# Prologue of a fused FFT filter and FFN: W_in loaded in seven pieces, x of batch 1 issued straight behind it, the imaginary filter cast on three engines, placements of F moved

## Chip, cores and metric

The kernel runs on one core of one Trainium2 chip. Times are device microseconds (us) of one execution. "Span" is the length of the profiled execution from its first to its last instruction; it is about 2 us shorter than that execution's time. Engines: PE (TensorE, matmuls), PEld (its weight loads), DVE (VectorE), ACT (ScalarE), POOL (GpSimd), SP (SyncE, which here issues the DMAs).

## The reference

```python
def _attn_ref(x, filt_r, filt_i):            # x: (8, 3008, 256), filters: (1505, 256)
    X = np.fft.rfft(x, axis=1)
    Y = X * (filt_r + 1j * filt_i)[None, :, :]
    return np.fft.irfft(Y, n=x.shape[1], axis=1).astype(np.float32)

def _moe_ref(x, w_in, w_out):                # x: (24064, 256), w_in: (256, 2048), w_out: (2048, 256)
    h = np.maximum(x @ w_in, 0.0)
    return (h * h @ w_out).astype(np.float32)
# reference: _moe_ref(_attn_ref(x, filt_r, filt_i).reshape(24064, 256), w_in, w_out)
```

## The kernel before

The Fourier transforms are matmuls. For each batch: a first transform (x to u, tile `psA`), u through memory (`dU`) into another order (`ut`), a second transform (`psB`), the product with the filter F (`prods`, `sF`), an inverse part (`psP`, evicted to `ze`), Z through memory (`dZ`, `zt`), a last inverse part (`psY` to `yt`). Then the FFN takes `yt` in groups of 512 tokens: `psH` = W_in times y, relu into `h`, square, `psO` = h times W_out. The FFN of one batch runs while the transform of the next is placed between its matmuls in a fixed order. Only batch 0, and three quarters of the first transform of batch 1, stand ahead of the FFN: that is the prologue, and only there does the change act.

The filters arrive with rows spread over partitions; `place_f` puts them in order with matmuls against permutation matrices and evicts the result to `sF`. `turn_u` does the same for u of batch 0 on chip.

```python
    def load_win(k):                       # W_in in two halves, in the buffers of x
        w32s[k] = p_x32.tile([128, DFF], F32, tag="x32", name=f"win32_{k}")
        nc.sync.dma_start(out=w32s[k], in_=moe_w_in[128 * k:128 * k + 128, :])

    def cast_win(k):
        for j in range(2):
            c = slice(1024 * j, 1024 * j + 1024)
            nc.gpsimd.tensor_copy(out=sWin[:, k, c], in_=w32s[k][:, c])
    # ... cut ...
    def unit_p0(k):                        # inverse part of batch 0: evict, write Z
        # ... cut: 8 matmuls into ps ...
        nc.scalar.copy(out=ze, in_=ps.rearrange("p t (a d) -> p (t a) d", d=D))
        nc.sync.dma_start(
            out=dZ[0].rearrange("(s p) d -> p s d", p=128)[:, 4 * k:4 * k + 4, :],
            in_=ze)
    # ... cut: the prologue ...
    for im, e in ((0, e0), (0, e1), (1, e0)):
        nc.gpsimd.tensor_copy(out=f16s[0][:, im, e], in_=f32s[im][:, e])
    # ... cut: sSPx, a copy of sSP with its halves swapped, on POOL ...
    for k in range(2):
        cast_win(k)
    uts[0] = p_ut.tile([128, NC, D], F16, tag="ut", name="ut_0")
    load_wide(1, 2)                        # x of batch 1, first third to be issued
    cast_wide(1, 2, nc.gpsimd, nc.gpsimd)
    for k in range(6):
        turn_u(k, nc.vector if k in (1, 3, 4, 5) else nc.scalar)
        if k > 2:
            place_f(0, k - 3, nc.scalar, True)
    nc.vector.tensor_copy(out=f16s[0][:, 1, e1], in_=f32s[1][:, e1])
    place_f(0, 3, nc.vector, True)
    place_f(1, 0, nc.scalar)
    for k in range(7):                     # "the loop"
        if k < 6:
            unit_b(0, 2 * k)
            if k < 5:
                place_f(1, k + 1, nc.scalar)
            unit_b(0, 2 * k + 1)
        if k > 0:
            unit_p0(k - 1)
        if k < 2:
            place_f(0, k + 4, nc.scalar)
        if k in (1, 2):                    # the other two thirds of x, behind writes of Z
            load_wide(1, k - 1)
            cast_wide(1, k - 1, nc.gpsimd, nc.gpsimd)
    read_z(0, 0)
    load_wout(0)
    read_z(0, 1)
    load_wout(1)
    for c in (0, 2, 1):
        chunk_a(1, c)                      # first transform of batch 1: 24 matmuls
    for c in (0, 2, 1):
        write_u(1, c)
    for n in range(4):
        unit_y(0, n)                       # first y, needs Z back from memory
    # ... cut: then the FFN, with the transforms of later batches between ...
```

## Time and profile before

| | before |
|---|---|
| median of 3 runs | 794.77 us (794.66 to 795.65) |
| the profiled execution | 797.61 us, span 795.8 us |
| PE busy | 783.1 us, 98% of the span |
| prologue, to the first relu `h` | 53.80 us |
| granted PE clock, 40 to 50 us | 0.66 |

### The profile page before, as it was taken

What the parts mean: (1) busy time and instruction counts of PE and PEld (TensorE: products, weight loads), DVE (VectorE), ACT (ScalarE), POOL (GpSimd) and SP (SyncE); (2) the same over time, 40 slices, a digit from 0 to 9 for tenths busy, and PEclk for the clock granted to TensorE, in tenths of its full rate; (3) what the DMA queues carried; (4) which work ended last, traced back from release to release, by engine and by line L of the source; (5) the groups of instructions that cost most, each with busy time, mean ns of one, the idle gap of its engine ahead of it and who ended that gap; (6) DMA issues with size and microseconds to landing.
All of it is one profiled execution on the core that took longest, in us unless ns stands there. A gap on an engine that the chain in (4) does not pass through costs nothing.

```text
span 795.8 us, 14801 instructions
## 1 busy us (share of the span) xinstructions
PE 783.1 (98%) x6102; PEld 553.7 (70%) x6102; DVE 552.2 (69%) x898; ACT 554.9 (70%) x708; POOL 24.4 (3%) x27
## 2 busy tenths in 40 slices
PE   8989999999999999999999999999999999999998
PEld 5846677667676676867778676776777667776666
DVE  6946995579855897559965699557985589554342
ACT  3856776767777677767777677676776767766664
POOL 3710000000000000000000000000000000000000
PEclk9989999999999999999999999999999999999999
DMA  9994555336724467055471555525563342511111
GB/s 352 361 277 134 130 151 139 92 126 165 202 58 107 158 165 181 30 164 151 124 183 49 171 153 137 129 71 156 156 170 97 87 142 80 123 48 41 40 41 54
DMA packets 88139, 107.32 MB, mean 135 GB/s; under 512 B 6288, under 2 KB 78864, under 8 KB 83856
## 3 DMA queue, kind: packets, MB, share of 16 engines
q1 hardware_dynamic: 87864, 106.19, 46.9%
q8 instruction: 48, 0.79, 0.4%
q10 hardware_dynamic: 144, 0.18, 0.1%
q14 instruction: 19, 0.16, 0.1%
q0 software_dynamic: 64, 0.00, 0.0%
HBM read 58.12 MB, written 48.23 MB: 134 GB/s over the span
## 4 chain that ended last, share of the span: by engine, by line
PE 93%; DMA 3%; ACT 1%; DVE 1%; issue 0%; POOL 0%; SPq 0%; ACTq 0%; DVEq 0%; POOLq 0%
PE psO L577 40%; PE psH L560 39%; PE psA L359 3%; PE psY L530 3%; PE psB L443 2%; PE psP L494 2%; PE warm L274 1%; DMA ut<-dU 1%; DMA xw<-in_x_dram 1%; PE psf L293 1%; DMA dZ<-ze 1%; ACT h L564 1%; PE psf L296 0%; DMA dU<-u 0%; PE psA L380 0%; ACT sF L303 0%
## 5 line engine op out<-in xcount | busy, mean ns | idle before, releaser
L564 ACT ACTIVATE h<-psH 128x1024 f16<-128x1024 f32 x376 | 385.2, 1025 | 189.7 <-PE psH L560 188.2
L577 PE MATMUL psO<-sWout,h 128*128 128x256 f16 x3008 | 388.6, 272 | 0.0
L560 PE MATMUL psH<-yt,sWin 128*128 128x512 f16 (+7 forms) x1728 | 386.9, 351 | 1.7 <-DVE yt L539 0.8
L577 PEld LDWEIGHTS <-h 128*128 128x128 f16 x3008 | 290.6, 98 | 77.3
L568 DVE TENSOR_TENSOR h<-h 128x1024 f16<-128x1024 f16 x376 | 253.7, 685 | 100.8 <-ACT h L564 99.2
L560 PEld LDWEIGHTS <-sWin 128*128 128x128 f16 x1728 | 159.5, 98 | 101.7 <-issue 3.5
L451 DVE TENSOR_TENSOR prod<-psB,sF 128x1024 f16<-128x1024 f32 x84 | 102.4, 1219 | 5.9 <-PE psB L443 5.6
L539 DVE CAST yt<-psY 128x376 f16<-128x376 f32 x62 | 33.9, 549 | 57.4 <-PE psY L530 57.4
L365 DVE CAST u<-psA 96x512 f16<-96x512 f32 x50 | 34.3, 687 | 47.3 <-PE psA L359 45.1
L496 ACT CAST ze<-psP 128x512 f16<-128x512 f32 x84 | 49.2, 586 | 17.8 <-PE psP L494 15.9
L588 ACT COPY ost<-psO 128x512 f32<-128x512 f32 (+1 forms) x96 | 55.7, 580 | 6.7 <-PE psO L577 5.3
L530 PEld LDWEIGHTS <-zt 112*128 112x128 f16 x512 | 34.9, 98 | 12.1 <-issue 2.0
L530 PE MATMUL psY<-sC,zt 112*128 112x94 f16 x512 | 42.3, 205 | 0.6 <-DMA zt<-dZ 0.3
L465 DVE TENSOR_TENSOR yf<-prod,yf 128x512 f16<-128x512 f16 x84 | 35.7, 425 | 2.9
L443 PE MATMUL psB<-ut,sSB 128*128 128x256 f16 x192 | 36.5, 272 | 0.6 <-DMA ut<-dU 0.5
L359 PE MATMUL psA<-x,sC 94*96 94x512 f16 x96 | 36.6, 382 | 0.0
L443 PEld LDWEIGHTS <-sSB 128*128 128x128 f16 x192 | 18.6, 98 | 20.9 <-issue 1.7
L494 PE MATMUL psP<-yf,sSP 128*128 128x256 f16 x168 | 32.1, 273 | 0.2 <-ACT yt L537 0.2
L537 ACT CAST yt<-psY 128x376 f16<-128x376 f32 x66 | 30.7, 468 | 1.1 <-PE psY L530 0.6
L338 DVE CAST x<-x 94x2048 f16<-94x2048 f32 x24 | 29.2, 1216 | 0.0
L363 ACT CAST u<-psA 96x512 f16<-96x512 f32 x50 | 28.6, 572 | 0.0
L458 DVE COPY yf<-prod 64x512 f16<-64x512 f16 x84 | 24.3, 289 | 2.9
(63 smaller groups left out, 255.9 us busy)
## 6 DMA issues: line engine op xcount, KB each, us to landing
x<-in_x_dram SPq DMA_DIRECT2D x20, 768.0 KB
zt<-dZ SPq DMA_DIRECT2D x64, 192.0 KB
dU<-u SPq DMA_DIRECT2D x28, 384.0 KB
dZ<-ze SPq DMA_DIRECT2D x28, 384.0 KB
out_dram<-ost SPq DMA_DIRECT2D x66, 128.0 KB
out_dram<-ost SPq DMA_DIRECT2D x31, 256.0 KB
ut<-dU SPq DMA_DIRECT2D x7, 1024.0 KB
xw<-in_x_dram SPq DMA_DIRECT2D x4, 1024.0 KB
```

What stands on the lines that cost most here:

```text
L359: nc.tensor.matmul(ps[0:96, :], sSA, x16s[(b, c)][:, m, :], start=True, stop=True)
L443: nc.tensor.matmul(ps[:, i * D:(i + 1) * D], sSB[:, 2 * p + i, :], uts[b][:, 2 * p + i, :], start=True, stop=True)
L451: nc.vector.tensor_mul(out=prod, in0=ps.rearrange("p (a d) -> p a d", d=D).unsqueeze(1).to_broadcast([128, 2, 2, D]), in1=sF[:, :, 2 * p:2 ...
L465: nc.vector.tensor_add(out=yf, in0=prod[:, 0], in1=yf)
L494: nc.tensor.matmul(ps[:, i * D:(i + 1) * D], sSP[:, 2 * p + i, :], yf[:, i, :], start=True, stop=True)
L496: nc.scalar.copy(out=zes[(b, c)][:, 2 * i6:2 * i6 + 2, :], in_=ps.rearrange("p (a d) -> p a d", d=D))
L530: nc.tensor.matmul(ps[:, 94 * jj:94 * jj + 94], zt[:, 4 * (g % 2) + jj, dt * 128:(dt + 1) * 128], sSY, start=True, stop=True)
L560: nc.tensor.matmul(ps[:, i, o:o + n], sWin[:, dt, jt * 128:(jt + 1) * 128], yts[b][:, dt, r:r + n], start=(dt == 0), stop=(dt == 1))
L564: nc.scalar.activation(out=h2[:, 2 * s:2 * s + 2, :], in_=ps, func=AF.Relu)
L568: nc.vector.tensor_mul(out=v, in0=v, in1=v)
L577: nc.tensor.matmul(pso[g][:, t % 2, :], h2s[g][:, jt, t * 128:(t + 1) * 128], sWout[:, jt, :], start=(jt == 0), stop=(jt == NJT - 1))
L588: nc.scalar.copy(out=ost[:, h0:h0 + step, :], in_=pso[g][:, h0:h0 + step, :])
```

## The change

Its intent is to have x of batch 1 on chip before PE comes to it. W_in no longer waits in the buffers of x: it is loaded in seven pieces into small buffers that stand idle in the prologue, and all of x of batch 1 is issued straight behind. The imaginary filter, which lands late, is cast by three engines at once, and two of the real placements move from the turns of u into the loop. The change also takes x of batch 0 whole again, which the kernel before loads and casts in halves.

```diff
-    def load_win(k):
-        w32s[k] = p_x32.tile([128, DFF], F32, tag="x32", name=f"win32_{k}")
-        nc.sync.dma_start(out=w32s[k], in_=moe_w_in[128 * k:128 * k + 128, :])
+    def load_win():
+        for k, c, n, pool, tag in ((0, 0, 768, p_ze, "ze"), (0, 768, 768, p_ze, "ze"),
+                                   (0, 1536, 512, p_prod, "prod"), (1, 0, 768, p_ze, "ze"),
+                                   (1, 768, 512, p_prod, "prod"), (1, 1280, 512, p_prod, "prod"),
+                                   (1, 1792, 256, p_yf, "yf")):
+            t = pool.tile([128, n], F32, tag=tag, name=f"win32_{k}_{c}")
+            nc.sync.dma_start(out=t, in_=moe_w_in[128 * k:128 * k + 128, c:c + n])
+            wins.append((t, k, slice(c, c + n)))
# ... cut: cast_win casts the pieces on POOL; place_f takes a list of engines; halves of x of batch 0 ...
-    for k in range(2):
-        load_win(k)
+    load_win()
+    for k in range(3):
+        load_wide(1, k)
# ... cut ...
-    for im, e in ((0, e0), (0, e1), (1, e0)):
-        nc.gpsimd.tensor_copy(out=f16s[0][:, im, e], in_=f32s[im][:, e])
+    for e in (e0, e1):
+        nc.gpsimd.tensor_copy(out=f16s[0][:, 0, e], in_=f32s[0][:, e])
+    turn_u(0, nc.scalar)
+    turn_u(1, nc.vector)
+    turn_u(2, nc.scalar)
+    turn_u(3, nc.vector)
+    place_f(0, 0, nc.scalar, rotate=True)
+    for eng, e in ((nc.vector, slice(0, 1024)), (nc.gpsimd, slice(1024, 2048)),
+                   (nc.scalar, slice(2048, QF))):
+        cast(eng, f16s[0][:, 1, e], f32s[1][:, e])
+    turn_u(4, nc.vector)
+    place_f(0, 1, nc.scalar, rotate=True)
+    turn_u(5, nc.vector)
+    place_f(1, 0, nc.scalar, nc.vector, rotate=True)
# ... cut: sSPx now in 12 pieces of 64x512 instead of 4 of 64x1536 ...
+    cast_win()
     for k in range(2):
-        cast_win(k)
-    uts[0] = p_ut.tile([128, NC, D], F16, tag="ut", name="ut_0")
-    load_wide(1, 2)
-    cast_wide(1, 2, nc.gpsimd, nc.gpsimd)
# ... cut: the old order of turns and placements ...
+        cast_wide(1, k, nc.gpsimd, nc.gpsimd)
     for k in range(7):
# ... cut ...
-        if k < 2:
-            place_f(0, k + 4, nc.scalar)
-        if k in (1, 2):
-            load_wide(1, k - 1)
-            cast_wide(1, k - 1, nc.gpsimd, nc.gpsimd)
+        if k < 4:
+            place_f(0, k + 2, nc.scalar)
+    cast_wide(1, 2, nc.vector, nc.scalar)
     read_z(0, 0)
```

More of the change, by code (lines that the diff above doesn't have):

```diff
@@ L210 @@
     xw32, xw16 = {}, {}
-    halves, later = ((0, 0), (0, 1)), []
     def load_wide(b, k):
@@ L218, in load_wide, with cast, cast_wide @@
         t = pool.tile([128, 8, D], F32, tag=tag, name=f"xw_{b}_{k}")
-        v = (v0[:, 0:8, :], v1, v0[:, 8:16, :])[k]
-        for m in (slice(0, 4), slice(4, 8)) if (b, k) in halves else (slice(0, 8),):
-            if m.stop > 4 and m.start == 4:
-                later.append((t, v, m))
-            else:
-                nc.sync.dma_start(out=t[:, m, :], in_=v[:, m, :])
-        xw32[(b, k)] = t
-    def cast_wide(b, k, *engs, parts=(0, 1)):
-        if 0 in parts:
-            xw16[(b, k)] = p_x16.tile([128, 8, D], F16, tag="x16", name=f"xw16_{b}_{k}")
-        for i in parts:
+        nc.sync.dma_start(out=t, in_=(v0[:, 0:8, :], v1, v0[:, 8:16, :])[k])
+        xw32[(b, k)] = t
+    def cast(eng, out, in_):
+        (eng.copy if eng is nc.scalar else eng.tensor_copy)(out=out, in_=in_)
+    def cast_wide(b, k, *engs):
+        t = p_x16.tile([128, 8, D], F16, tag="x16", name=f"xw16_{b}_{k}")
+        for i in range(2):
             m = slice(4 * i, 4 * i + 4)
-            engs[i].tensor_copy(out=xw16[(b, k)][:, m, :], in_=xw32[(b, k)][:, m, :])
-    for k in range(2):
+            cast(engs[i], t[:, m, :], xw32[(b, k)][:, m, :])
+        xw16[(b, k)] = t
+    for k in range(3):
         load_wide(0, k)
-    for t, v, m in later:
-        nc.sync.dma_start(out=t[:, m, :], in_=v[:, m, :])
-    load_wide(0, 2)
     f32s = []
@@ L276, with place_f @@
     f16s = []
-    def place_f(im, k, eng, rotate=False):
+    def place_f(im, k, *engs, rotate=False):
         if rotate:
@@ L299, in place_f @@
             n = t.shape[1]
+            eng = engs[i % len(engs)]
             dst = sF[:, im, 4 * k + 2 * i:4 * k + 2 * i + 2 * n, :]
@@ L311, with cast_win @@
     w32s = {}
-    def load_win(k):
-        w32s[k] = p_x32.tile([128, DFF], F32, tag="x32", name=f"win32_{k}")
-        nc.sync.dma_start(out=w32s[k], in_=moe_w_in[128 * k:128 * k + 128, :])
-    def cast_win(k):
-        for j in range(2):
-            c = slice(1024 * j, 1024 * j + 1024)
-            nc.gpsimd.tensor_copy(out=sWin[:, k, c], in_=w32s[k][:, c])
+    def load_win():
[6 more added lines that the diff above has]
+            wins.append((t, k, slice(c, c + n)))
+    def cast_win():
+        for t, k, c in wins:
+            nc.gpsimd.tensor_copy(out=sWin[:, k, c], in_=t)
+    wins = []
     def load_wout(k):
@@ L390, in chunk_a, with chunk_a0 @@
                     eng.tensor_copy(out=o, in_=pv)
-    def chunk_a0(c, ks):
-        for k in ks:
+    def chunk_a0(c):
+        for k in range(2):
             banks, groups = bank_pair(f"psA_0_{c}_{k}")
@@ L653 @@
     uT = p_h2.tile([128, 2, NC, 128], F16, tag="h2", name="uT")
-    for i in range(2):
-        for k in range(2):
-            cast_wide(0, k, nc.vector, nc.vector, parts=(i,))
-    cast_wide(0, 2, nc.vector, nc.gpsimd)
+    for k in range(3):
+        cast_wide(0, k, nc.vector, nc.gpsimd if k == 2 else nc.vector)
     def load_const(t, d, k):
@@ L666 @@
         load_const(sSP[:, c, :], dSP, k)
-    for k in range(2):
-        load_win(k)
-    for k in range(2):
-        for c in (0, 2):
-            chunk_a0(c, (k,))
-    for k in range(2):
-        for c in (1, 3):
-            chunk_a0(c, (k,))
+    load_win()
+    for k in range(3):
+        load_wide(1, k)
+    for c in (0, 2, 1, 3):
+        chunk_a0(c)
     f16s.append(p_h2.tile([128, 2, QF + D], F16, tag="h2", name="f16"))
@@ L678 @@
         nc.gpsimd.tensor_copy(out=f16s[0][:, im, QF:], in_=nyq[:, im, :])
-    for im, e in ((0, e0), (0, e1), (1, e0)):
-        nc.gpsimd.tensor_copy(out=f16s[0][:, im, e], in_=f32s[im][:, e])
-    for k in range(2):
-        sSPx.append(p_u.tile([128, 12, 128], F16, tag="u", name=f"sSPx_{k}"))
-        c = slice(12 * k, 12 * k + 12)
-        nc.gpsimd.tensor_copy(out=sSPx[k][0:64], in_=sSP[64:128, c, :])
-        nc.gpsimd.tensor_copy(out=sSPx[k][64:128], in_=sSP[0:64, c, :])
-    for k in range(2):
-        cast_win(k)
-    uts[0] = p_ut.tile([128, NC, D], F16, tag="ut", name="ut_0")
-    load_wide(1, 2)
-    cast_wide(1, 2, nc.gpsimd, nc.gpsimd)
-    for k in range(6):
-        turn_u(k, nc.vector if k in (1, 3, 4, 5) else nc.scalar)
-        if k > 2:
-            place_f(0, k - 3, nc.scalar, True)
-    nc.vector.tensor_copy(out=f16s[0][:, 1, e1], in_=f32s[1][:, e1])
-    place_f(0, 3, nc.vector, True)
-    place_f(1, 0, nc.scalar)
+    for e in (e0, e1):
+        nc.gpsimd.tensor_copy(out=f16s[0][:, 0, e], in_=f32s[0][:, e])
+    uts[0] = p_ut.tile([128, NC, D], F16, tag="ut", name="ut_0")
+    turn_u(0, nc.scalar)
[10 more added lines that the diff above has]
+    place_f(1, 0, nc.scalar, nc.vector, rotate=True)
+    for k in range(6):
+        if k % 3 == 0:
+            sSPx.append(p_u.tile([128, 12, 128], F16, tag="u", name=f"sSPx_{k}"))
+        c, o = slice(4 * k, 4 * k + 4), slice(4 * k % 12, 4 * k % 12 + 4)
+        nc.gpsimd.tensor_copy(out=sSPx[-1][0:64, o, :], in_=sSP[64:128, c, :])
+        nc.gpsimd.tensor_copy(out=sSPx[-1][64:128, o, :], in_=sSP[0:64, c, :])
+    cast_win()
+    for k in range(2):
+        cast_wide(1, k, nc.gpsimd, nc.gpsimd)
     for k in range(7):
```

## The prediction

> **What bounds the kernel now.** I read the page first, then the busy time by stretches, then the chain of waits of the first 60 us, then the timelines of PE, ACT, POOL and the DMA queue there.
>
> The page says that TensorE is the bound nearly everywhere:
>
> ```profile
> PE 783.1 (98%) x6102; PEld 553.7 (70%) x6102; DVE 552.2 (69%) x898; ACT 554.9 (70%) x708; POOL 24.4 (3%) x27
> ```
>
> POOL has work only in the prologue, before the FFN starts at 52.5 us, and every line of the change is in that prologue. The stretches show where PE loses time there (columns: length, busy us and instructions of PE, PEld, DVE, ACT, POOL, granted clock, DMA share, GB/s):
>
> ```profile
> 20.00:30.00 10.00, 9.64 (x100) 8.21 (x98) 8.93 (x11) 7.74 (x9) 7.50 (x6) 1.00 1.03 424
> 30.00:40.00 10.00, 9.28 (x89) 7.89 (x87) 9.79 (x9) 8.99 (x9) 7.92 (x8) 1.00 0.84 295
> 40.00:50.00 10.00, 8.07 (x26) 4.03 (x26) 2.36 (x4) 3.59 (x5) 2.03 (x2) 0.66 0.84 246
> 140.00:160.00 20.00, 20.00 (x145) 13.31 (x143) 11.66 (x19) 14.77 (x21) 0.00 (x0) 1.00 0.32 87
> ```
>
> In 40 to 50 us PE issues only 26 matmuls at a mean clock of 0.66; later it is full at clock 1.00. The chain of waits names the cause of the hole:
>
> ```profile
> 34.44 7.08 DMA xw<-in_x_dram
> 41.64 1.05 POOL xw L232
> 42.74 0.58 PE psA L380
> 43.32 0.43 PE psA L378
> ...
> 48.85 0.23 PE psA L380
> ```
>
> The last third of x of batch 1 is issued at 34.44 and lands at 41.52, POOL casts its first half to 42.70, and only then does the first transform of batch 1 (24 matmuls of 512 columns, L378/L380) run, at 0.43 us each instead of 0.22. The DMA queue shows why the load starts so late:
>
> ```profile
> 31.97 0.34 SPq L224 DMA_DIRECT2D xw<-in_x_dram  x1
> 33.96 0.38 SPq L483 DMA_DIRECT2D dZ<-ze  x1
> 34.44 0.45 SPq L224 DMA_DIRECT2D xw<-in_x_dram  x1
> ```
>
> Both loads use the buffers in which W_in waits for its cast (POOL, 29.92 to 33.86), and they stand behind the first writes of Z in the queue. In 30 to 32 us the DMA share is down to 0.48.
>
> **What the Trainium skill says.** "TensorE: Matmul & The Clock Gate", Part 1, has the array at half rate after about one idle window of 3.4 us and back at full rate after about one busy window. The trace agrees: the granted clock is 0.50 from 42 to 48 us, about two such windows, after a stretch (38.5 to 41.9 us) with nine matmuls, and 1.00 from 50 us. "DMA: Bandwidth & Descriptors", Specifications, names a fabric ceiling of 435 GB/s; the trace has 424 in 20 to 30 us, so the early loads can only be put in another order, not made faster. The same page, Anatomy of one DMA, puts a fixed 2.0 us on a transfer before its semaphore (it states this for the GpSimd path). The last write of Z is issued at 41.9 and the reads of Z finish issuing at 44.92, in fair agreement. "GPSIMD Engine Reference", Specifications, says that GpSimd shares its SBUF interface with VectorE: the x cast on POOL at 12.01 took 1.56 us beside a DVE cast, against 1.04 later.
>
> **The change, part by part.**
>
> (a) W_in in seven pieces in buffers that stand idle in the prologue; x of batch 1 all three thirds issued straight behind it. This removes the waits for W's cast and for writes of Z. The bytes are the same. Up to 30 us the trace has moved 10 x (286 + 418 + 424) kB = 11.3 MB. All constants, filters, x of batch 0, W_in and the whole x of batch 1 come to about 13.6 MB (my sum of the tile sizes). The other 2.3 MB at 424 GB/s take 5.4 us: x is complete at about 35.5 us, the first two thirds near 33. That is 6 to 8 us earlier than 41.5.
>
> (b) POOL. It now does f (1024 columns, with DVE beside it, so till about 22.9), then the swapped copies as 12 of 64x512, W_in as 7, then four x casts. Its timeline gives start to start 1.00 us for 1024 columns, 1.42 for 1504 and 0.375 for 256, so about 0.17 fixed plus 0.81 per 1000. Twelve copies at 0.62 make 7.4 us from 23.7 (before: 6.2) to 31.1; W_in 4096 columns and seven fixed parts 4.5 to 35.6; four x casts 4.0 to 39.6. So the cast that PE needed at 42.70 is there at 38.6, its second half at 39.6. The last third is cast by DVE (0.69) and ACT (about 1.0) after the loop.
>
> (c) f of the imaginary part on three engines. It lands at 21.36 (POOL's start). Before: 1.44 on POOL, then a DVE part that began only at 23.07 behind six evictions, so PE placed it at 23.9. Now all three parts are done at about 22.9: PE starts 1.0 us sooner, and ACT evicts this first placement at 23.9 instead of 24.99. In turn DVE and ACT sit still until 21.4 with evictions behind them, which I find repaid.
>
> (d) Placement of F. Two of the real placements (ACT L303 1.02, DVE L307 1.21) go from the turns of u into the loop, both to ACT. The argument that gives half of the first imaginary one to DVE has no effect: the order of instructions shows one ACT instruction of 1024 columns there, since its bank pair is one group. Now ACT bounds the loop. Before, from the eviction at 24.99 to this one, eleven evictions later:
>
> ```profile
> 34.07 1.11 ACT L303 ACTIVATE sF<-psf,sign 128x1024 f16<-128x1024 f32 x1
> 35.16 1.01 ACT L482 CAST ze<-psP 128x1024 f16<-128x1024 f32 x1
> 36.31 1.11 ACT L303 ACTIVATE sF<-psf,sign 128x1024 f16<-128x1024 f32 x1
> 37.40 1.01 ACT L482 CAST ze<-psP 128x1024 f16<-128x1024 f32 x1
> ```
>
> that is 12.41 / 11 = 1.13 us each. The order of instructions puts 12 evictions between the first imaginary placement and the end of the last, where before ten did: 23.9 + 12 x 1.13 = 37.4 start, 38.5 end (before 36.31 and 37.42). The last two products on DVE (1.164 us each: 13.97 / 12) need it: 40.9, against 40.16 before. So (c) and (d) together make the loop end 0.7 us later.
>
> (e) The end of the prologue. PE finishes the last inverse part at 41.4 (before 40.65) and finds x there. 24 matmuls at 0.2175 make 5.2 us: the end is at 46.6 instead of 50.65, 4.0 us sooner. But the next work on PE, the first part of y, needs Z back through memory. The last eviction of Z ends at 42.4 (before 41.86), its write lands near 45, the second read is issued at 45.2 and lands, with 2.4 us for it as an estimate, at 47.6. Before, this was hidden: y started at 50.77. So y starts 3.2 us sooner, and this trip is what ends last. The FFN behind it has the same instructions and PE is full, so the gain is kept to the end. With a Z trip a bit quicker on the now emptier DMA engines I take 3.4 us: 794.77 - 3.4 = 791.4.
>
> **The rivals.**
>
> Rival 1, the clock falls all the same. In the last loop turns PE still waits for products. For: the clock fell before. Against: then PE had some 1.1 us of matmuls in 3.4 us, now I count about 2.2 (8 + 4 + 8 matmuls of 256 columns at 0.11). If it falls for one window, 15 or 16 of the 24 matmuls run slow: 1.7 us or more is added, and y starts near 49; for two windows the gain is about 1 us: 792.5 to 794.
>
> Rival 2, ACT doesn't bound the loop, as evictions follow one another more closely than 1.13, or DVE stays the bound from its earlier start (first product 24.9 + 13.97 = 38.9). Then all is 1 to 2 us sooner: 789.5 to 790.5. Against: eviction takes 1.02 or 1.11 by itself.
>
> Rival 3, POOL or the DMA is later than I have it: smaller pieces, more issues (0.34 us each), the copies of W standing ahead of x. It has 1.8 us in hand (39.6 against 41.4); if 3 us late, PE waits over 1 us and perhaps loses the clock too: 793 to 795.
>
> Rival 4, a new wait in the first FFN turns: W_out's load is issued behind the Z reads, so barely earlier, while its casts come 3 us earlier. Before, DVE found it there at 58.51, some 12 us after its issue; I expect no wait. If there is one: up to 2 us lost.
>
> **Range and chances.** The main line is 791.4, rival 2 pulls down by 1.5, rivals 1, 3 and 4 up by 1 to 3. I give the main line and its neighbourhood 0.6, faster still 0.15, and 0.25 to the three that eat the gain. That makes 789.3 to 793.8 with 8 in 10. 2% is 15.9 us; the whole hole in PE from 38 to 50 us is not that long, and nothing added costs as much. So within 2%: 0.985, faster 0.01, slower 0.005.
>
> **What would show each step.** (a) x of batch 1 issued before 27 us and landed by 36; POOL no longer waits for it. (b) POOL's last x cast ends near 39.6. (c) The first imaginary placement on PE near 22.9. (d) ACT evicts without pause from 24 to 38, DVE waits for ACT's sF in the loop, the last product ends near 40.9. (e) L378/L380 at 0.22 us each and no clock below 0.9 in 40 to 50; a wait of about 1 us for Z before the first y; the FFN's first matmul near 49.1 instead of 52.5. I am wrong if the clock is still 0.5 there, if PE still waits for POOL, or if the gain at the FFN's start is not found at the end.

## More of the kernel before

What the prologue is worth is read where it ends; the chain of waits of the kernel before (start, length, engine, tile, line) has there

```profile
51.78 0.18 PE psY L530 x4
...
53.80 1.03 ACT h L564
```

From that first `h<-psH` on no pause of PE in this trace is above 0.51 us.

## The result

| | before | after |
|---|---|---|
| median | 795.21 us (794.66 to 796.75, 4 runs) | 796.61 us (796.17 to 797.94, 4 runs) |
| ratio after / before | | 1.0017, 95% interval 0.9998 to 1.0037 |
| the profiled execution | 797.61 us, span 795.8 | 796.17 us, span 794.3 |

A ratio is the mean time of one kernel's fast runs over that of the other's of the same rounds, so it is not quite the ratio of the medians. The predicted gain of 3.4 us would be a ratio of 0.9958; that is outside the interval, and 796.61 is outside the predicted range. Yet the two profiled executions, taken by themselves, show a gain of 1.4 us. The rest of this document is about that contradiction.

In this trace the prologue did most of what was predicted of it. The busy time by stretches of the kernel after (columns as in the prediction: length, then busy us and instructions of PE, PEld, DVE, ACT, POOL, granted clock, DMA share, GB/s):

```profile
20.00:30.00 10.00, 9.24 (x96) 7.94 (x94) 9.73 (x10) 9.11 (x11) 7.73 (x12) 1.00 1.04 406
30.00:40.00 10.00, 9.28 (x85) 7.68 (x83) 8.05 (x8) 9.22 (x9) 8.97 (x13) 1.00 0.88 327
40.00:50.00 10.00, 7.74 (x54) 4.71 (x54) 5.74 (x8) 5.94 (x9) 0.00 (x0) 1.00 0.76 216
```

In 40 to 50 us PE issues 54 matmuls at full clock where it issued 26 at 0.66. The queue of SP (start, length, what) shows the loads of x ahead of the first write of Z:

```profile
24.63 2.30 SPq L218 DMA_DIRECT2D xw<-in_x_dram  x3
28.69 13.71 SPq L485 DMA_DIRECT2D dZ<-ze  x6
```

POOL's timeline shows W_in and the four casts of x, with no wait for a load:

```profile
30.75 4.39 POOL L320 CAST sWin<-win 128x768 f16<-128x768 f32 x7
35.08 4.00 POOL L222 CAST xw<-xw 128x1024 f16<-128x1024 f32 x4
```

The last cast ends at 39.08 (predicted 39.6). The chain of waits is now the one that the prediction named: last products, inverse part, eviction, the trip of Z through memory, FFN.

```profile
37.97 2.35 DVE prods L453 x2
...
40.37 0.61 PE psP L482 x4
...
41.00 1.02 ACT ze L484
...
42.04 2.37 DMA dZ<-ze
...
50.82 1.01 ACT h L566
```

PE's own timeline of the kernel after has the price of that trip: it waits 1.32 us for Z (predicted about 1), and the FFN starts at 49.54 (predicted 49.1).

```profile
48.09 0.33 PE L532 MATMUL psY<-sC,zt 112*128 112x94 f16 x4 [1.32 <-DMA zt<-dZ]
...
49.54 1.82 PE L562 MATMUL psH<-yt,sWin 128*128 128x512 f16 x7 [0.28 <-ACT yt L539]
```

So in this pair of traces the first `h` goes from 53.80 to 50.80: 3.0 us of the 3.4. But the stretch behind it, from the first `h` to the start of the last matmul, which has the same work, takes 738.37 us in the kernel before and 739.74 in the kernel after. The busy time by stretches finds a large part of this in one place. Before:

```profile
630.00:700.00 70.00, 70.00 (x515) 48.62 (x514) 52.68 (x90) 50.55 (x64) 0.00 (x0) 1.00 0.41 114
```

After:

```profile
630.00:700.00 70.00, 68.91 (x515) 47.95 (x514) 52.30 (x90) 49.35 (x63) 0.00 (x0) 1.00 0.41 112
```

PE stands still for 1.09 us there, 580 us behind the last line that the change touches. The waits of PE between 63 and 790 us (engine, line, what was waited for: us in all, times, longest) name it. Before:

```profile
PE psB L443 <- DMA ut<-dU: 0.5, 1, 0.5
```

After:

```profile
PE psB L445 <- DMA ut<-dU: 1.9, 4, 1.1
```

The longest, 1.09 us, is at 641 us, where the second transform of the last batch waits for its u.

### The profile page after: what moved, and what is told of

It reads as the page before. It is cut to its first block, busy times and chain, and to the rows that moved or that the text cites. A ratio compares the mean times of both kernels' runs of the same rounds, so it can differ in the third digit from the quotient of the medians.

```text
span 794.3 us, 14824 instructions
## 1 busy us (share of the span) xinstructions
PE 779.9 (98%) x6102; PEld 552.5 (70%) x6102; DVE 552.2 (70%) x897; ACT 557.7 (70%) x711; POOL 23.7 (3%) x36
## 4 chain that ended last, share of the span: by engine, by line
PE 90%; DMA 6%; DVE 1%; ACT 1%; SPq 0%; issue 0%; DVEq 0%; ACTq 0%
PE psO L579 40%; PE psH L562 38%; PE psA L361 3%; PE psB L445 3%; PE psY L532 3%; DMA ut<-dU 2%; PE psP L496 2%; DMA f<-in_filt_i_dram 2%; DMA dU<-u 1%; DMA zt<-dZ 1%; PE psf L287 1%; PE psf L290 1%; ACT h L566 1%; ACT sF L298 0%; DVE h L570 0%; DVE prods L453 0%
```

## The experiments

All ratios are against the kernel before, run in the same rounds on the same chip. Kernels "before" and "after" were also run unchanged, since a prediction of 3 us in 795 stands or falls with how alike two runs of one kernel are. Two questions stand behind the twelve runs: is the prologue of the kernel before always as slow as in the one profile that the prediction was made from (the first theory, T1: it is not, and the subtraction was made from the wrong base), and is the gain that is left lost again in the stretch behind (the rival)?

### before_again: the kernel before, unchanged

No edit.

> The kernel before, unchanged, to see what its ordinary runs look like. Theory T1 (the profile of before that the prediction rests on was an exception: its clock fell to 0.50 for 6.8 us just when the first transform of batch 1 ran, and the timed runs lack that): most runs have a granted clock of 0.998 to 1.000 and a span near 793 us (about 1.8 under the time), and in the profile L378/L380 take 0.22 us each, with the FFN's first ACT instruction (h<-psH) near 51 us instead of 53.8. Theory T2 (the fall of the clock is there in every run, so the changed kernel really starts its FFN 3 us sooner and loses that later, in waits for u of later batches): clock 0.996, span 795.8, first h<-psH at 53.8 again.

Measured: 795.01 us median (793.99 to 796.59), ratio 0.9991 (0.9974 to 1.0009). The busy time by stretches of its trace:

```profile
40.00:50.00 10.00, 7.80 (x52) 4.55 (x50) 5.64 (x7) 5.46 (x9) 2.61 (x3) 1.00 0.78 232
```

The clock does not fall: 1.00 where the first trace had 0.66, and 52 matmuls where that had 26. The first `h` is at 52.09, not 53.80. It would have been sooner still, but the loop of this run ends 1.6 us later. The trace points to DVE and POOL. DVE's timeline:

```profile
23.48 2.19 DVE L695 CAST f<-f 128x1504 f16<-128x1504 f32 x1
```

POOL's timeline of the same run:

```profile
23.42 1.46 POOL L684 COPY sSPx<-sSP 64x1536 f16<-64x1536 f16 x1 [0.92 <-DMA sSP<-cSP]
```

In the first trace of the kernel before DVE's cast started first:

```profile
23.07 0.93 DVE L695 CAST f<-f 128x1504 f16<-128x1504 f32 x1
```

There POOL's copy started 0.66 us behind it. The one that starts second waits for the other: the cast takes 0.93 us where it leads, 2.19 us where it is 0.06 us behind. The Trainium skill, "SBUF — State Buffer", Terms, says this of the port pair that the two engines share: it is held for the full instruction and "the loser **fully blocks**". The traces agree. In four other traces with this order of casts (before_noz, before_third, before_fill, x_only) the cast leads and takes 0.93 us; in before_fill POOL's copy starts 0.21 us behind it and takes 2.05 us instead of 1.46.

With the clock full, this run shows another thing that the first trace hid: PE waits for Z ahead of the first y in the kernel before, too.

```profile
49.39 0.33 PE L530 MATMUL psY<-sC,zt 112*128 112x94 f16 x4 [0.55 <-DMA zt<-dZ]
```

So here the trip of Z ended last already, and PE's wait for x (0.72 us) lay hidden behind it. What follows: the base of the prediction's subtraction is not a constant of the kernel.

### before_third: the kernel before, a third time

No edit; run later, on another chip.

> The kernel before once more, for a third trace of it. Theory T1: the granted clock stays 1.00 in 40 to 50 us (a fall there is the exception), first h<-psH at 50.5 to 52.1. The DVE cast of F takes 0.93 us if it begins ahead of POOL's swapped copy and about 2.2 if it begins just behind it; in the latter case the last product begins near 40.6 instead of 39.

Measured: 797.16 us (795.62 to 797.78), ratio 1.0000 (0.9981 to 1.0019); first `h` at 52.76. The stretches:

```profile
40.00:50.00 10.00, 7.35 (x31) 3.79 (x30) 3.15 (x4) 4.25 (x6) 2.02 (x2) 0.83 0.77 226
```

The clock fell again, but for one window of 3.41 us (42.92 to 46.33) instead of two (6.83 us). So the fall is not an exception, as I had come to believe after before_again: it came in two of three traces, for two windows, none and one. The timed runs say the same, since the record has the granted clock of each, as a mean over the run (0.998 in this trace, with one window; 0.996 in the first, with two). Of the 56 runs of the kernel before in the four later rounds, 30 have 0.998 or less and take 797.4 us on average; the other 26 take 795.1. The mean start of `h` over the three is 52.88 us.

### after_again: the kernel after, unchanged

No edit.

> The changed kernel unchanged, a second trace. If what it loses behind the FFN's start is bound to the kernel: PE waits again about 1 us for u of the last batch near 641 us and the stretch from first h<-psH to the last matmul is 739.7 or more. If that was chance: no such wait, the stretch near 738.5, time near 795.

Measured: 796.42 us (794.73 to 797.92), ratio 1.0004 (0.9985 to 1.0023). The first `h` is at 50.73 (50.80 in the first trace), and PE again waits for u at 641 us, 1.35 us this time. Its waits from 63 to 790 us:

```profile
PE psB L445 <- DMA ut<-dU: 1.9, 3, 1.3
```

So both the gain and what is lost later come again. With the unchanged kernels' traces side by side:

| trace | first `h` | first `h` to last matmul | span |
|---|---|---|---|
| before | 53.80 | 738.37 | 795.8 |
| before_again | 52.09 | 739.04 | 794.8 |
| before_third | 52.76 | 739.52 | 795.9 |
| mean of before | 52.88 | 738.98 | 795.5 |
| after | 50.80 | 739.74 | 794.3 |
| after_again | 50.73 | 740.59 | 795.1 |
| mean of after | 50.77 | 740.17 | 794.7 |

On average the prologue gives 2.1 us, the stretch behind takes 1.2 back, and the tail behind the last matmul 0.1 more: 0.8 us are left.

### before_noz and after_noz: no trip of Z ahead of the first y

The first two reads of Z take a constant instead, so the output is wrong, with the same bytes and shapes. The edit is the same in both:

```diff
         for k in ks:
+            if b == 0 and c == 0:
+                nc.sync.dma_start(out=zt[64 * k:64 * k + 48],
+                                  in_=dSB.ap()[48 * k:48 * k + 48, 0:2048].rearrange("q (j d) -> q j d", d=D))
+                continue
```

> The kernel before with the first two reads of Z (for y of the first rows of batch 0) taken from a constant in memory, so that they wait for nothing; wrong result on purpose. T1 (Z's trip through memory ends about when the first transform of batch 1 does, once the clock is full): gain of 0 to 0.7 us. T2: gain of 0, y waits for the slow transform alone.

> The changed kernel with the same two reads of Z taken from a constant; wrong result on purpose. T1 and the prediction's step (e): the trip of Z is what ends last in the changed kernel's prologue, so the first h<-psH comes at 49.1 to 49.4 instead of 50.8, and the time falls by 1.3 to 1.8 us against the changed kernel (796.6), to near 795. If the trip is hidden: no gain.

Measured: before_noz 795.08 us (794.58 to 796.43), ratio 0.9992 (0.9976 to 1.0008); after_noz 796.01 us (795.41 to 796.33), ratio 1.0000 (0.9984 to 1.0017). In after_noz the first `h` comes at 49.76, 1.04 us sooner than in the kernel after: the trip of Z is what ends last there, as predicted. Its stretch from first `h` to last matmul is 740.85 us, and its median is 0.6 us under the 796.61 of the kernel after (which ran in other rounds), a difference that the spread doesn't resolve. In before_noz the first `h` is at 50.55, but not for the sake of Z: its trace waits 1.88 us for x and the clock stays full. It is one more trace of this prologue in which the clock did not fall (in two of its six timed runs it is 0.997 and 0.998).

### before_fill: keeping PE busy in the hole

Nine idle matmuls of 512 columns ahead of the reads of Z in the kernel before, to hold the clock without moving any load.

```diff
+    ps = psO("fill").rearrange("p a d -> p (a d)")
+    for _ in range(9):
+        nc.tensor.matmul(ps, zero, sF[:, 0, 0:2, :], start=True, stop=True)
     read_z(0, 0)
```

> The kernel before with nine idle matmuls (zeros, 512 columns) on PE just ahead of the first transform of batch 1, to keep the clock up while x is awaited. T1: the clock stays 1.00, first h<-psH near 51, time the same as before within 0.1% since ordinary runs have full clock anyway. T2: 2.5 to 3 us faster than before (ratio 0.9965).

Measured: 797.5 us (796.29 to 799.05), ratio 1.0023 (1.0005 to 1.0040). The clock stayed at 1.00, the first transform ran at its full rate (42.84 to 48.4), and the first `h` is at 51.56, 1.3 us ahead of the mean of before. Yet the time rose, and I had expected no such thing. Its waits from 63 to 790 us:

```profile
PE psB L443 <- DMA ut<-dU: 1.4, 1, 1.4
```

One wait of 1.43 us for u, but at 261 us: the same thing as in the kernel after, at another batch. An edit that adds nothing but PE instructions in the prologue moves a wait that stands hundreds of us behind. That pointed to something that goes by the count of PE's instructions.

### What lies under the wait for u

At each batch the SP queue writes four parts of u and then reads them back. I take the interval from the issue of the fourth write to the issue of the read as the time the write takes to land. The SP timeline has it; in the kernel before, last batch:

```profile
635.77 0.33 SPq L342 DMA_DIRECT2D dU<-u  x1
639.06 0.98 SPq L434 DMA_DIRECT2D ut<-dU  x2
```

In the kernel after:

```profile
632.89 0.33 SPq L344 DMA_DIRECT2D dU<-u  x1
637.24 0.80 SPq L436 DMA_DIRECT2D ut<-dU  x2
```

That is 3.29 us before and 4.35 us after. The DMA view of the kernel after, of the 2.5 us that follow that write's issue, shows a packet of another queue beside it (queue: packets, MB, share of the 16 engines' time):

```profile
q1 hardware_dynamic: 705, 0.36, 56.2%
q8 instruction: 1, 0.02, 2.3%
```

In the same 2.5 us the kernel before has only q1 packets. Over a whole execution the page counts

```profile
q8 instruction: 48, 0.79, 0.4%
```

0.79 MB in 48 packets are 16 KB each, and 2 x 6102 matmul and weight-load instructions over 48 are 254 for each packet: this queue brings PE's instructions. The Trainium skill, "Runtime: NRT & Kernel Launch", Instruction fetch mechanics, says that instructions are refilled in 16 KiB blocks of 256 over a queue of the sequencer's own, and calls it mostly hidden. The packets agree. No wait of PE is put down to them; but one such packet takes 0.88 to 1.69 us in these traces, on the same 16 DMA engines, by the profile's count, as the packets of u.

I took this interval for the seven batches of all fourteen traces, 98 writes (the first batch of x_c3 and x_c3_warm52 left out, as more writes stand ahead there: 96). Four of them have a refill that starts 1.16 to 2.16 us after the write's issue, and these take 4.10 to 4.68 us. The other 92 take 3.26 to 3.84 us. The limits are read off these writes; they are no rule. The packet times in the traces show the hold-up itself: of the 768 packets of the last batch's fourth write, 17 (after), 19 (after_again) and 18 (after_noz) start more than 3.05 us after its issue, and none in the three traces of before.

| trace, batch | refill starts after the write by | write to read |
|---|---|---|
| before, last | 2.71 us | 3.29 us |
| before_again, last | 2.66 us | 3.28 us |
| before_third, last | 2.63 us | 3.30 us |
| after, last | 2.00 us | 4.35 us |
| after_again, last | 2.16 us | 4.54 us |
| after_noz, last | 1.55 us | 4.10 us |
| before_fill, third of the seven | 1.16 us | 4.68 us |
| before_fill, last | 0.51 us | 3.38 us |

This does not cover every wait for u: after_noz also waits 1.17 us at 259 us, where the write took 3.76 us and a refill starts 3.20 us after its issue. It may have met the read behind the write; no run tests that.

In the kernel after PE also has two more semaphore instructions than before (42 for 40), from another pattern of waits, and the order of its work is another. So its refills, one per 256 instructions, fall elsewhere against the work. This was so far only argued from traces; the next two runs test it.

### after_warm52: the refills moved by 26 pairs of instructions

The 26 idle matmuls of 512 columns with which the kernel opens become 52 of 256 columns: the same columns, 26 matmuls and 26 weight loads more in PE's program.

```diff
-    for _ in range(26):
-        nc.tensor.matmul(ps, zero, sF[:, 0, 0:2, :], start=True, stop=True)
+    for _ in range(52):
+        nc.tensor.matmul(ps[:, 0:256], zero, sF[:, 0, 0, :], start=True, stop=True)
```

> The changed kernel with 52 warm-up matmuls of 256 columns in place of 26 of 512: the same PE time, but PE's program is 52 instructions longer ahead of everything, which shifts where in the program PE's instruction buffer is refilled (16 KB each, 48 transfers in a run, by DMA). Theory C (the wait near 641 us is a write of u held up by such a refill on one of its 16 DMA engines): the refill comes 3 to 5 us sooner relative to that write, the write lands 3.3 us after its issue instead of 4.35, and PE's wait there is gone; waits may come elsewhere. If the wait is from something else, it stays at 641 us with 1.1 us.

Measured: first `h` at 50.72, as in the kernel after. The refill now starts 1.10 us before the issue of the last batch's fourth write, 3.1 us sooner than in the kernel after, as expected; the write takes 3.41 us (no packet of it starts late), and the wait at 641 is gone. Waits from 63 to 790 us:

```profile
PE psB L445 <- DMA ut<-dU: 0.3, 2, 0.2
```

The stretch from first `h` to last matmul is 739.28 us, 0.9 less than the mean of the two unchanged runs of after; 0.52 us is now lost on a wait for Z at 691 us. The time is 796.1 us (795.55 to 797.77), ratio 1.0001 (0.9984 to 1.0018), against 796.42 and 1.0004 for after_again in the same rounds: the right way, and not resolved.

### after_warm24: the refills moved by two pairs

```diff
-    for _ in range(26):
+    for _ in range(24):
```

> The changed kernel with 24 warm-up matmuls in place of 26: PE's program is four instructions shorter ahead of everything. The changed kernel has 42 semaphore instructions on PE where before has 40, so its refill boundaries lie two instructions sooner in the work; in its three traces the refill fell 1.6 to 2.2 us after the issue of the last batch's last write of u and held it up, in the three of before 2.6 to 2.7 us after it, and it didn't. Theory C': with four fewer the refill falls at 2.6 us or later, the write lands in 3.3 us, PE's wait near 641 is 0.3 us or less, the stretch from first h<-psH to the last matmul is 739.4 or less; first h<-psH stays near 50.7. If two instructions aren't the cause, the wait of over 1 us stays.

Measured: 795.37 us (794.78 to 796.59), ratio 0.9993 (0.9969 to 1.0016). With four instructions fewer the refill starts 2.69 us after the last batch's fourth write instead of 2.00. The SP timeline:

```profile
634.26 0.33 SPq L344 DMA_DIRECT2D dU<-u  x1
637.67 0.80 SPq L436 DMA_DIRECT2D ut<-dU  x2
```

The write takes 3.41 us, and PE's wait there 0.24 us instead of 1.09 or 1.35. This edit takes instructions away and the other adds them; both move the refill off the write, and both times the wait goes. With before_fill, which brings such a wait to a batch that had none, I call the cause of this wait shown. What it does to the time of the timed runs is not: neither edit's ratio differs clearly from that of the kernel after. In this run the clock fell for one window (50.20 to 53.61) behind PE's wait of 1.38 us for Z: first `h` at 51.59. So Rival 1 of the prediction does come, in one of the five traces of the kernel after and its variants (after_noz among them), and, by the granted clock, in 3 of the 10 timed runs of the kernel after.

### x_only: W_in and x alone

The kernel before with parts (a) and (b): W_in in pieces, x of batch 1 straight behind, and the casts that go with them; the order of F and its casts as before, and sSPx in its four large copies. The edit is these parts of the diff above; f_only below has the parts (c) and (d). Neither has sSPx in pieces or x of batch 0 taken whole, so the two do not add up to the change.

```diff
-    for k in range(2):
-        load_win(k)
+    load_win()
+    for k in range(3):
+        load_wide(1, k)
# ... cut: load_win and cast_win as in the change ...
-        if k in (1, 2):
-            load_wide(1, k - 1)
-            cast_wide(1, k - 1, nc.gpsimd, nc.gpsimd)
+    cast_wide(1, 2, nc.vector, nc.scalar)
     read_z(0, 0)
```

> The kernel before with only the loads changed: W_in in seven pieces, x of batch 1 loaded straight behind it, cast as in the changed kernel; F's casts and placement as before. Theory A (x's wait is hidden behind Z's trip once the clock is full): no wait of L380's group for POOL, the transform of batch 1 ends about 1.5 to 2.5 us sooner than in an ordinary run of before, but y waits over 1 us for Z and the FFN's first h<-psH comes 10.5 to 12 us after the last product on DVE begins, about as in before (11.5 in before_again, 14.9 in the profile of before). Time within 0.2% of before. Theory B (the early loads disturb others): something later than before in the prologue, first h<-psH after 52.

Measured: 794.85 us (794.22 to 797.54), ratio 0.9990 (0.9970 to 1.0010), span 792.7. First `h` at 49.88, the clock full, and PE waits 1.44 us for Z: in this one trace, the whole gain of the prologue and 0.9 us more than the full change. It comes 11.4 us after the start of the last product, where before_again, with x late but the clock full, has 11.5: theory A of the expectation, that the wait for x is hidden behind Z's trip once the clock is full, fits. The stretch behind is 739.02 us, as in the kernel before, and the refill stands 2.63 us behind the last batch's write, which lands in 3.40.

### f_only: the casts and the order of F alone

```diff
+    for eng, e in ((nc.vector, slice(0, 1024)), (nc.gpsimd, slice(1024, 2048)),
+                   (nc.scalar, slice(2048, QF))):
+        cast(eng, f16s[0][:, 1, e], f32s[1][:, e])
# ... cut: turns and placements in the order of the change ...
-        if k < 2:
-            place_f(0, k + 4, nc.scalar)
+        if k < 4:
+            place_f(0, k + 2, nc.scalar)
```

> The kernel before with only F changed: cast on three engines, placement between the turns of u and in the loop; loads as before. Theory A: last product on DVE begins near 39.1 as in the changed kernel, x still comes at 42 to 43 (PE waits 1 to 2 us), the first h<-psH at 50.5 to 52 with a full clock, time within 0.2% of before. The DVE part of the cast takes 1.5 us rather than 0.69, since POOL begins its part first. Theory B (F's placement is what cost the time): slower than before by over 0.2%, last product later than 40.

Measured: 795.49 us (794.93 to 796.79), ratio 0.9994 (0.9977 to 1.0010). First `h` at 51.49; its last product starts at 39.81, in x_only at 38.52. So parts (c) and (d) make the loop end later. One reason stands in DVE's timeline of the kernel after; f_only has the same 1.51 us:

```profile
20.49 1.51 DVE L222 CAST f<-f 128x1024 f16<-128x1024 f32 x1 [0.17 <-DMA f<-in_filt_i_dram]
```

POOL's part of the cast started 0.07 us sooner:

```profile
20.42 1.04 POOL L222 CAST f<-f 128x1024 f16<-128x1024 f32 x1 [2.31 <-DMA f<-in_filt_i_dram]
```

DVE's part waits for it and takes 1.51 us instead of the 0.69 it takes alone. The imaginary filter is cast at 22.0, and the evictions on DVE behind it start some 0.8 us later than they could (an estimate, 1.51 - 0.69). The other reason, argued from the prediction and not tested alone, is ACT's two extra evictions in the loop.

### x_c3: a version that uses what was learned

The trip of Z is what ends the prologue, and PE stands still for 1.4 us in it. So the last quarter of the first transform of batch 1, which the FFN's turns carried until now, goes into that hole: 8 matmuls of 512 columns. This is x_only, with sSPx in 12 pieces as in the change (so that POOL lets its buffers go in time) and

```diff
-        u = p_u.tile([96, 8, D], F16, tag="u", name=f"u_{b}_{c}")
+        pool, tag = (p_x16, "x16") if c == 3 else (p_u, "u")
+        u = pool.tile([96, 8, D], F16, tag=tag, name=f"u_{b}_{c}")
# ... cut ...
-        for a in range(12 if b == 1 else 0, 16):
+        for a in range(16 if b == 1 else 0, 16):
# ... cut ...
-    for c in (0, 2, 1):
+    for c in (0, 2, 1, 3):
         chunk_a(1, c)
-    for c in (0, 2, 1):
+    for c in (0, 2, 1, 3):
         write_u(1, c)
```

> The kernel with only the loads changed (x_only), plus: the swapped copies on POOL in 12 pieces, so that a DVE cast never waits over 0.6 us for one of them; and the last quarter of the first transform of batch 1 (8 matmuls, 1.74 us of PE) moved from the FFN's first turns into the wait for Z that x_only showed (1.43 us). If Z's trip is what ends last, PE finds that work for nothing: wait for Z below 0.3 us, first h<-psH at 50.0 to 50.4, and the first psO matmul comes 1.3 us sooner relative to it; span near 791.5, time 793.3, ratio to before 0.997. If the rest is ruled by where the refills of PE's instructions fall, up to 1 us of it goes again.

Measured: correct, 793.12 us (792.52 to 794.00), ratio 0.9952 (0.9933 to 0.9970), span 791.0. The stretches:

```profile
40.00:50.00 10.00, 9.31 (x63) 5.70 (x62) 6.47 (x9) 6.84 (x10) 0.01 (x1) 1.00 0.74 217
```

PE is busy 9.31 of 10 us there, 7.74 in the kernel after. The first `h` is at 50.57, 0.7 us later than in x_only, and the stretch behind is 736.63 us, 2.4 shorter, of which the work moved out of it is 8 x 0.2175 = 1.7. PE waits nowhere more than 0.31 us after 124 us. This kernel and its variant below are the only ones here whose interval stands clear of 1 on the fast side. It does not overlap that of the kernel after in either of its rounds, though those were on other chips. Part of the lead is the base: 8 of the 11 runs of before in its rounds have a clock of 0.998 or less. The other three take 795.4 us on average, x_c3's six, none of them below 0.999, 793.2.

### x_c3_warm52: the same with its refills moved

The warm-up edit of after_warm52, on x_c3.

> The same with 52 warm-up matmuls of 256 columns for 26 of 512, which in the changed kernel took away the held-up write of u of the last batch. Expected: prologue as in x_c3; behind the FFN's start no wait of PE for u over 0.5 us; span 791 to 792, ratio to before 0.996 to 0.998.

Measured: 794.81 us (793.59 to 795.96), ratio 0.9971 (0.9950 to 0.9992). First `h` at 50.62, as in x_c3, but the stretch behind takes 738.50 us instead of 736.63. PE waits 0.74 us for u at 354 us and 0.68 us for Z at 213 us. At the former a refill starts 3.81 us after the write's issue, that is just behind the issue of the read. So the place of the refills is luck for any such kernel: moved blindly, they may cost as much as a change in the prologue gains.

## Why the prediction was wrong

**What held.** The wait for x of batch 1 went, the clock stayed full in the profiled run, ACT came to bound the loop (DVE waits for ACT 0.97 and 0.98 us in it, by the trace for the eviction `ze`, where the prediction named `sF`), and the trip of Z became what ends the prologue; after_noz shows this last by taking the trip away. Rival 3 (POOL or the loads late) did not come. Rival 4 (a wait for W_out) did not show among the waits. "Within 2%" was right.

**The sizes in the prologue.** The last product ended 0.2 us later than before, not the 0.7 of (d), since the last of F's placements was evicted at 37.63, not 38.5. The trip of Z from the end of its last eviction (42.02) to the first y (48.09) took 6.1 us where I had 5.2: the write as expected (2.37 us from issue to landing), the read longer than the 2.4 us I gave it. Together: 3.0 us gained in this pair of traces where I had 3.4. This step was nearly right.

**Failed step 1: "794.77 - 3.4 = 791.4".** The 3.4 us are read from a trace, and the trace is of an execution that took 797.61 us, not 794.77. In that one the clock was at half for two windows. In the second trace of the same kernel it did not fall, in the third for one window, and the first `h` stood at 53.80, 52.09 and 52.76. Against their mean the change brings 2.1 us forward, not 3.0 or 3.4.

What was wrong in the prologue is the sentence of (e) that the trip of Z was hidden before: it was hidden only behind the slow transform. The first `h` comes 14.8 and 14.5 us after the start of the last product in the two traces with a fall; with x as late but the clock full, 11.5 (before_again), 11.7 (f_only) and 12.2 (before_noz, where nothing waits for Z); with x early, 11.4 to 11.7 (after, after_again, x_only). So at full clock the wait for x was worth 0.9 us at most in these traces; the rest of the loss was the fall. The timed runs agree: 794.77 is about the 795.1 of the runs of before without a fall, and at a clock of 0.999 or more the kernel after is no faster (795.8 us, 4 runs, against 795.4, 6 runs, in the rounds of after_again).

I took the largest of the three losses and subtracted it from the median of runs that need not have had it. From the execution that the loss was read in, the same sum gives 797.61 - 3.4 = 794.2.

**Failed step 2: "the FFN behind it has the same instructions and PE is full, so the gain is kept to the end".** The stretch from first `h` to last matmul is 738.98 us on average before and 740.17 after. Most of the 1.2 us, 1.09 and 1.35 in the two traces of after, is one wait of PE for u at 641 us, which the kernel before hasn't. It comes from a refill of PE's instructions that shares the DMA engines with the last part of u. That the place of the refill decides is shown by after_warm24, after_warm52 and, the other way round, before_fill. That the change moved it there is a matter of where 256-instruction blocks happen to end. No view I had read would have given that.

**The sum.** By the traces 3.4 becomes 2.1 at the first `h`, less 1.2 behind it, less 0.1 in the tail: 0.8 us, a ratio of 0.999. That is within the interval of the second rounds (0.9985 to 1.0023), and 0.0008 under that of the first (0.9998 to 1.0037).

**What stays open.** Single runs of one kernel spread widely: the kernel before from 793.67 to 799.51 us over the chips here, much of it along with the granted clock. An interval of 0.2% is 1.6 us, so the times tell neither 0.8 us from nothing, nor x_only from after; these readings rest on traces, some of them on one trace. The profiled runs are not the median ones either. Why the clock falls in one run and not in the next isn't settled: no run of f_only, where x comes late, is below 0.999 either. And the 1.4 us between the two medians of the first rounds, against 0.2 in the second, are not explained by anything that I saw in a trace. That the first rounds' runs of before had mostly the full clock would fit them, but their clocks are not on record.

## What to carry to other kernels

A gain read from one profile must be subtracted from the time of that very execution; take a second and third profile of the kernel before, and look at the granted clock of its timed runs, above all where the lost time holds a fall of the clock or a race of two engines for a port. A kernel that is full of one engine's work is not thereby insensitive to what comes before: with waits of a few tenths of a us in hand at each trip through memory, anything that moves the refills of instructions against such trips, even idle matmuls, can cost or give a us hundreds of us later, so check the stretches behind the change for new waits before you believe or deny a gain of 0.2%. A wait that lies beside another which ends about as late is worth little by itself. Once it is removed, look for what now ends last and give the engine that waits for it work that it would do later anyway: x_c3, which does so, is the fastest kernel here, part of its lead being the luck of its refills.

## What the Trainium skill lacked or had wrong

- "Runtime: NRT & Kernel Launch", Instruction fetch mechanics, calls the refill mostly hidden. For PE it is. It lacks what a 16 KB packet can cost a transfer of the kernel: where one started 1.16 to 2.16 us after the issue of a 384 KB write, the write took 4.10 to 4.68 us (4 cases); the other 92 took 3.26 to 3.84 us.
- "GPSIMD Engine Reference", Specifications, which the prediction used, names the sharing, and contention with some DVE instructions, but not who pays. That is no gap of the skill as a whole: the lock of "SBUF — State Buffer", Terms, is what the traces show. Its price here for a start 0.06 or 0.07 us later was 2.19 us for 0.93, and 1.51 us for 0.69.
- "TensorE: Matmul & The Clock Gate", Part 1, has the fall of the clock after at least one idle window of about 3.4 us. Here it fell behind waits of PE of 1.71 us (before), 2.65 us (before_third) and 1.38 us (after_warm24), each with thin PE work around it, and did not fall behind 1.88 us (before_noz), 1.44 us (x_only) and 1.32 us (after). The length of a fall, 3.41 or 6.83 us, agrees with its window.
- "DMA: Bandwidth & Descriptors", Anatomy of one DMA, gives 2.0 us for a transfer's fixed part on the GpSimd path. On SP's queue the whole write of Z (128x1024 f16, 262 KB) took 2.37 us (after) and 2.42 us (before_again) from its issue to its landing. For that path the page has a first-byte latency, but no time to the semaphore.
